# q, k and v cast to fp16 by GpSimd's DMA queue as they are loaded, in an attention kernel followed by a feed-forward network

## The chip, the cores and the metric

The kernel runs on one core of a Trainium2 chip. The metric is device time in microseconds of one execution; less is better. The kernel before was run three times: 346.05, 347.59 and 348.84 us, median 347.59.

## What is computed

Attention with a causal sliding window of 64 over 8 batches of 8 heads, 576 positions, head size 64, and then a feed-forward network with a squared ReLU on the 4608 resulting rows of 512:

```python
rel = pos[:, None] - pos[None, :]
mask = (rel >= 0) & (rel < 64)
scores = np.where(mask, q @ k.T / sqrt(64), -1e9)
attn = softmax(scores) @ v             # per batch and head
x = attn.transpose(0, 2, 1, 3).reshape(4608, 512)
h = np.maximum(x @ w_in, 0.0)          # w_in 512 x 2048
out = (h * h @ w_out)                  # w_out 2048 x 512
```

All inputs and the output are fp32 in memory; the kernel computes with fp16 operands.

## The kernel before, in words

The 4608 rows are 36 chunks of 128 positions, and four chunks are a group; there are nine groups. A chunk is two blocks of 64 positions. Each block of 64 queries needs 128 keys: its own block and the one before it.

A chunk goes through these functions. `load` (L144) brings k, q and v of the chunk, 128 positions x 8 heads x 64, from fp32 memory into three staging tiles of a pool of fifteen (`stage`), through DMAs on SP's queue (L151; for four of the chunks, which span two batches, in two halves at L154 and L156). GpSimd (POOL) then casts k and q to fp16 (L160, L162) and v to the tile `v_ev` (L164). The values of the first block of a chunk need v shifted by 64 positions, so two more POOL copies (L165, L167) put the lower half of `v_ev` into the upper half of `v_od` of this chunk, and its upper half into the lower half of `v_od` of the next. There are eight pairs of v tiles (`NV`) and eight fp16 tiles each for k and q. `transposes` (L169) turns k and q on TensorE and copies them to kT (DVE, L180, L177) and qT (ACT, L182). `scores` (L185) multiplies, takes the exponential on ACT (L199) and applies the mask as a minimum with 0 or 65504 on DVE (L201). `values` (L204) multiplies by v with a column of ones, and divides by the sum on DVE (L215, L216). `to_xT` (L221) transposes the result into xT (DVE, L226).

`ffn_up` and `ffn_up_chunk` multiply xT by w_in (TensorE L250, or L271 by single chunks), ReLU on ACT, squaring on DVE (L255, L276). `ffn_out` multiplies by w_out (L296), scales on ACT (L301) and stores through SP's queue (L303).

The weights are loaded as fp32 through SP's queue into four shared staging tiles (`ws`), w_in in 16 pieces of 256 KB (L115), cast on DVE (L117), and w_out in 16 pieces (L129), cast on POOL (L130). The masks are built by POOL in `base` (L75 to L80) and copied on DVE (L87). `warm` (L282) issues matmuls of no use for the result between the steps of chunk 0.

The program is written as one sequence: load of chunk 0, w_in, loads of chunks 1 to 6, the steps of chunk 0 with `warm` between them, load of chunk 7, w_out, then the steps of chunks 1 to 7 with their parts of the first product (L311 to L326), and from then on nine rounds (L329) in which `ffn_out` of one group, `ffn_up` of the next, `attention` of the one after and the loads two groups ahead are woven together. A scheduler of the language then orders the instructions of each engine by its own estimates, so that the order on an engine is not simply that of the text; it also places the waits. [...]

The functions that the diff touches:

Of the kernel before, what the change touches and what calls it, by code (L numbers as in the profile page):

```python
# [9 lines left out]
FP32 = mybir.dt.float32  # L10
FP16 = mybir.dt.float16
# [16 lines left out]
def kernel(  # L28
# [9 lines left out]
    nc = tc.nc  # L38
    B, H, S, D = q.shape
    NT, DM = out.shape  # L40
    DFF = moe_w_in.shape[1]
    P = 128
    HP = H // 2
    NCK = NT // P
    NB = S // 64
# [6 lines left out]

    const = ctx.enter_context(tc.tile_pool(name="const", bufs=1))
    wst = ctx.enter_context(tc.tile_pool(name="wst", bufs=4))
    stage = ctx.enter_context(tc.tile_pool(name="stage", bufs=15))
    st16 = ctx.enter_context(tc.tile_pool(name="st16", bufs=8))
    attw = ctx.enter_context(tc.tile_pool(name="attw", bufs=3))
    smallp = ctx.enter_context(tc.tile_pool(name="smallp", bufs=4))
# [18 lines left out]
        out=base[:], in_=base[:], compare_op=ALU.is_ge, fill=0.0, base=-1,  # L77
# [3 lines left out]
        out=base[:], in_=base[:], compare_op=ALU.is_ge, fill=0.0, base=64,  # L81
# [19 lines left out]
    NV = 8  # L101
    v_evs = [const.tile([P, H, 66], FP16, name=f"v_ev{i}") for i in range(NV)]
    v_ods = [const.tile([P, H, 66], FP16, name=f"v_od{i}") for i in range(NV)]
# [38 lines left out]
    q16s, k16s, qTs, kTs, pms, xs = {}, {}, {}, {}, {}, {}  # L142

    def load(i):  # L144

        sts = []
        for (src, nm) in ((k, "k"), (q, "q"), (v, "v")):
            st = stage.tile([P, H, D], FP32, name=f"{nm}_st", tag="st")
            b0, j0 = divmod(2 * i, NB)
            if j0 + 1 < NB:  # L150
                nc.sync.dma_start(  # L151
                    out=st[:], in_=src[b0, :, 64 * j0:64 * j0 + P, :].rearrange("h p d -> p h d"))
            else:
                nc.sync.dma_start(  # L154
                    out=st[0:64], in_=src[b0, :, 64 * j0:S, :].rearrange("h p d -> p h d"))
                nc.sync.dma_start(  # L156
                    out=st[64:P], in_=src[b0 + 1, :, 0:64, :].rearrange("h p d -> p h d"))
            sts.append(st)
        k16s[i] = st16.tile([P, H * D], FP16, name="k16", tag="k16")
        nc.gpsimd.tensor_copy(out=k16s[i][:], in_=sts[0][:].rearrange("p h d -> p (h d)"))  # L160
        q16s[i] = st16.tile([P, H * D], FP16, name="q16", tag="q16")
        nc.gpsimd.tensor_copy(out=q16s[i][:], in_=sts[1][:].rearrange("p h d -> p (h d)"))  # L162
        v_ev, v_od, v_next = v_evs[i % NV], v_ods[i % NV], v_ods[(i + 1) % NV]
        nc.gpsimd.tensor_copy(out=v_ev[:, :, 0:D], in_=sts[2][:])  # L164
        nc.gpsimd.tensor_copy(out=v_od[64:P, :, 0:D], in_=v_ev[0:64, :, 0:D])  # L165
        if i + 1 < NCK:
            nc.gpsimd.tensor_copy(out=v_next[0:64, :, 0:D], in_=v_ev[64:P, :, 0:D])  # L167

    def transposes(i):  # L169
        ps = ps_att.tile([P, 2, HP, P], FP16, name="qkT_ps", tag="ps_a")  # L170
        for s, src in enumerate((k16s, q16s)):
            for hp in range(HP):
                nc.tensor.transpose(out=ps[:, s, hp, :], in_=src[i][:, hp * P:(hp + 1) * P],  # L173
                                    identity=ident[:])
        kT = attw.tile([P, HP, 192], FP16, name="kT", tag="kT")
        if i > 0:
            nc.vector.tensor_copy(out=kT[:, :, 0:64], in_=kTs[i - 1][:, :, P:192])  # L177
        else:
            nc.vector.memset(kT[:, :, 0:64], 0.0)
        nc.vector.tensor_copy(out=kT[:, :, 64:192], in_=ps[:, 0])  # L180
        qT = attw.tile([P, HP, P], FP16, name="qT", tag="qT")
        nc.scalar.activation(out=qT[:], in_=ps[:, 1], func=AF.Copy, scale=1.0)  # L182
        kTs[i], qTs[i] = kT, qT
# [44 lines left out]
    def attention(g):  # L228

        steps = []  # L230
        fns = (transposes, scores, values, to_xT)
        for t in range(4 + len(fns) - 1):
            for s, fn in enumerate(fns):
                if 0 <= t - s < 4:
                    steps.append(lambda fn=fn, i=4 * g + t - s: fn(i))
        return steps

    def loads(g):
        return [lambda i=i: load(i) for i in range(4 * g, 4 * g + 4)]
# [69 lines left out]


    load(0)  # L311
    for s in load_w_in():
        s()
    NFIRST = 8
    for i in range(1, NV - 1):
        load(i)
    T, S_, V, X = [lambda i, fn=fn: fn(i) if i < NFIRST else None
                   for fn in (transposes, scores, values, to_xT)]
    T(0), warm(6), S_(0), warm(6), V(0), warm(6), X(0), warm(4)
    load(NV - 1)  # L320
# [48 lines left out]
```

The softmax here doesn't subtract the row's maximum and nothing guards it: scores larger than these inputs give would overflow.

## Time and profile before

| | |
|---|---|
| profiled execution, its span from first to last instruction | 345.9 us |
| three timed executions | 346.05, 347.59, 348.84 us |
| TensorE busy | 324.3 us (94%) |
| DVE busy | 207.9 us (60%) |
| ACT busy | 163.8 us (47%) |
| POOL busy | 121.5 us (35%) |
| DMA on SP's hardware queue, share of 16 engines | 51.7% |
| bytes moved | 46.65 MB |

The page gives no time for the profiled execution other than its span, so the span is set beside the three timed executions. PE is TensorE, PEld its weight loads, DVE VectorE, ACT ScalarE, POOL GpSimd, SP the engine that issues the DMAs; a q after the name is the engine's queue. In a slice view, each digit is the busy share of one fortieth of the span in tenths. In a timeline row, the first number is the start in us, the second the length in us; what stands in square brackets is the idle time before it and what ended it. L with a number is the line in the kernel.

### The profile page before, as it was taken

What the parts mean: (1) busy time and instruction counts of PE and PEld (TensorE: products, weight loads), DVE (VectorE), ACT (ScalarE), POOL (GpSimd) and SP (SyncE); (2) the same over time, 40 slices, a digit from 0 to 9 for tenths busy, and PEclk for the clock granted to TensorE, in tenths of its full rate; (3) what the DMA queues carried; (4) which work ended last, traced back from release to release, by engine and by line L of the source; (5) the groups of instructions that cost most, each with busy time, mean ns of one, the idle gap of its engine ahead of it and who ended that gap; (6) DMA issues with size and microseconds to landing.
All of it is one profiled execution on the core that took longest, in us unless ns stands there. A gap on an engine that the chain in (4) does not pass through costs nothing.

```text
span 345.9 us, 7917 instructions
## 1 busy us (share of the span) xinstructions
PE 324.3 (94%) x3146; PEld 178.2 (52%) x3146; DVE 207.9 (60%) x506; ACT 163.8 (47%) x289; POOL 121.5 (35%) x204
## 2 busy tenths in 40 slices
PE   1957888999999999999999999999999999999995
PEld 0346787875555555445545554455445544544442
DVE  2656988852666776676776657665675566544400
ACT  1123457544535646643664466436544654444411
POOL 4009895497753333316566544530000000000000
PEclk9996999999999999999999999999999999999998
DMA  7799987899972455546877757730011000000021
GB/s 200 249 252 239 234 247 252 207 230 228 243 172 61 93 121 123 121 124 155 212 185 182 170 135 184 185 87 27 23 45 36 30 32 32 30 30 32 35 88 62
DMA packets 122341, 46.65 MB, mean 135 GB/s; under 512 B 113600, under 2 KB 113600, under 8 KB 122304
## 3 DMA queue, kind: packets, MB, share of 16 engines
q1 hardware_dynamic: 122304, 46.15, 51.7%
q8 instruction: 24, 0.39, 0.5%
q14 instruction: 13, 0.11, 0.1%
HBM read 36.70 MB, written 9.44 MB: 133 GB/s over the span
## 4 chain that ended last, share of the span: by engine, by line
PE 83%; DVE 7%; DMA 5%; ACT 2%; SPq 1%; issue 1%; ACTq 0%
PE ops L296 37%; PE hps L250 28%; DMA ws<-in_moe_w_in_dram 5%; PE qkT_ps L173 4%; PE av L211 4%; PE xt_ps L224 2%; DVE h_397 L276 1%; DVE h_1087 L276 1%; DVE xT L226 1%; DVE w_in_sb L117 1%; PE hps_639 L271 1%; SPq L151 1%; SPq L115 0%; PE hps_1088 L271 0%; PE hps_1537 L271 0%
## 5 line engine op out<-in xcount | busy, mean ns | idle before, releaser
L250 PE MATMUL hps<-xT,w_in_sb 128*128 128x512 f16 x448 | 115.2, 379 | 0.0
L254 ACT ACTIVATE hrelu<-hps 128x512 f32<-128x512 f32 x112 | 66.8, 598 | 91.6 <-PE hps L250 90.9
L250 PEld LDWEIGHTS <-w_in_sb 128*128 128x128 f16 x448 | 43.7, 98 | 52.6 <-issue 0.3
L271 PEld LDWEIGHTS <-w_in_sb 128*128 128x128 f16 x512 | 31.2, 99 | 8.2 <-issue 3.9
L301 ACT ACTIVATE osb<-ops 128x512 f32<-128x512 f32 x36 | 21.6, 600 | 29.1 <-PE ops L296 28.9
L182 ACT ACTIVATE qT<-qkT_ps 128x512 f16<-128x512 f16 x36 | 21.5, 596 | 22.6 <-DVE kT L180 22.3
L216 DVE TENSOR_TENSOR x_sb<-av,rden 128x256 f16<-128x256 f32 x72 | 27.5, 415 | 0.1
L180 DVE COPY kT<-qkT_ps 128x512 f16<-128x512 f16 x36 | 15.2, 421 | 18.0 <-PE qkT_ps L173 17.8
L226 DVE COPY xT<-xt_ps 128x512 f16<-128x512 f16 x36 | 15.1, 420 | 12.7 <-PE xt_ps L224 12.7
L215 DVE RECIPROCAL rden<-av 128x4 f32<-128x4 f32 x72 | 11.4, 178 | 17.1 <-PE av L211 17.1
L255 DVE SCALAR_TENSOR_TENSOR h_5222<-hps,hrelu 128x512 f16<-128x512 f32 x16 | 11.1, 691 | 16.6 <-ACT hrelu L254 16.6
L296 PE MATMUL ops<-w_out_sb,h_1087 128*128 128x512 f16 x64 | 17.5, 380 | 0.0
L191 PEld LDWEIGHTS <-kT 64*128 64x128 f16 x576 | 11.0, 95 | 12.2 <-issue 9.6
L296 PE MATMUL ops<-w_out_sb,h_3120 128*128 128x512 f16 x64 | 16.5, 380 | 0.0
L296 PE MATMUL ops<-w_out_sb,h_2579 128*128 128x512 f16 x64 | 16.5, 380 | 0.0
L296 PE MATMUL ops<-w_out_sb,h_4199 128*128 128x512 f16 x64 | 16.5, 380 | 0.0
L296 PE MATMUL ops<-w_out_sb,h_3658 128*128 128x512 f16 x64 | 16.5, 380 | 0.0
L296 PE MATMUL ops<-w_out_sb,h_2041 128*128 128x512 f16 x64 | 16.5, 380 | 0.0
L296 PE MATMUL ops<-w_out_sb,h_4736 128*128 128x512 f16 x64 | 16.4, 379 | 0.0
L296 PE MATMUL ops<-w_out_sb,h_397 128*128 128x512 f16 x64 | 15.3, 380 | 0.0
L224 PE MATMUL xt_ps<-ident,x_sb 128*128 128x128 f16 x144 | 15.1, 222 | 0.1
L255 DVE SCALAR_TENSOR_TENSOR h_4736<-hps,hrelu 128x512 f16<-128x512 f32 x16 | 11.0, 689 | 6.8 <-ACT hrelu L254 6.4
(837 smaller groups left out, 611.1 us busy)
## 6 DMA issues: line engine op xcount, KB each, us to landing
out_dram<-osb SPq DMA_DIRECT2D x36, 256.0 KB, 2.2
k_st<-in_k_dram SPq DMA_DIRECT2D x32, 256.0 KB, 3.9
q_st<-in_q_dram SPq DMA_DIRECT2D x32, 256.0 KB, 4.0
v_st<-in_v_dram SPq DMA_DIRECT2D x32, 256.0 KB, 4.1
ws<-in_moe_w_in_dram SPq DMA_DIRECT2D x16, 256.0 KB, 4.2
k_st<-in_k_dram SPq DMA_DIRECT2D x8, 128.0 KB, 3.2
q_st<-in_q_dram SPq DMA_DIRECT2D x8, 128.0 KB, 3.0
v_st<-in_v_dram SPq DMA_DIRECT2D x8, 128.0 KB, 3.2
```

The lines of the kernel that those rows point to most:

```text
L173: nc.tensor.transpose(out=ps[:, s, hp, :], in_=src[i][:, hp * P:(hp + 1) * P], identity=ident[:])
L180: nc.vector.tensor_copy(out=kT[:, :, 64:192], in_=ps[:, 0])
L182: nc.scalar.activation(out=qT[:], in_=ps[:, 1], func=AF.Copy, scale=1.0)
L216: nc.vector.tensor_tensor(out=x_sb[:, 4 * half:4 * half + 4, :], in0=av[:, :, 0:D], in1=rden[:].to_broadcast([P, 4, D]), op=ALU.mult)
L224: nc.tensor.transpose(out=xt[:, c, :], in_=xs[i][:, 2 * c:2 * c + 2, :], identity=ident[:])
L226: nc.vector.tensor_copy(out=xT_of(i // 4)[:, :, (i % 4) * P:(i % 4 + 1) * P], in_=xt[:])
L250: nc.tensor.matmul(hps[:], w_in_sb[:, c, f * P:(f + 1) * P], xT_of(g)[:, c, :], start=(c == 0), stop=(c == DMC - 1))
L254: nc.scalar.activation(out=hrelu[:], in_=hps[:], func=AF.Relu)
L255: nc.vector.scalar_tensor_tensor(out=h2s[g][:, f, :], in0=hps[:], scalar=0.0, in1=hrelu[:], op0=ALU.max, op1=ALU.mult)
L271: nc.tensor.matmul(hps[:, f, :], w_in_sb[:, c, (4 * fq + f) * P:(4 * fq + f + 1) * P], xT_of(g)[:, c, t0:t0 + P], start=(c == 0), stop=(c ...
L296: nc.tensor.matmul(hold["ps"][:], h2s[g][:, f, ts * P:(ts + 1) * P], w_out_sb[:, f, :], start=(f == 0), stop=(f == FFC - 1))
L301: nc.scalar.activation(out=osb[:], in_=hold["ps"][:], func=AF.Copy, scale=OUT_SCALE)
```

## The change

k, q and v are no longer loaded as fp32 through SP's queue and cast by POOL instructions. The loads are issued on POOL's DMA queue with an fp16 destination, so that the cast happens in the transfer; v goes straight into `v_ev`. The two shifted copies of v become SBUF to SBUF transfers on SP's queue. The staging pool is gone. The transposes read k and q through a three-dimensional tile instead of a flat one.

```diff
-    stage = ctx.enter_context(tc.tile_pool(name="stage", bufs=15))
...
     def load(i):
 
-        sts = []
-        for (src, nm) in ((k, "k"), (q, "q"), (v, "v")):
-            st = stage.tile([P, H, D], FP32, name=f"{nm}_st", tag="st")
-            b0, j0 = divmod(2 * i, NB)
+        v_ev, v_od, v_next = v_evs[i % NV], v_ods[i % NV], v_ods[(i + 1) % NV]
+        k16s[i] = st16.tile([P, H, D], FP16, name="k16", tag="k16")
+        q16s[i] = st16.tile([P, H, D], FP16, name="q16", tag="q16")
+        b0, j0 = divmod(2 * i, NB)
+        for (src, dst) in ((k, k16s[i]), (q, q16s[i]), (v, v_ev[:, :, 0:D])):
             if j0 + 1 < NB:
-                nc.sync.dma_start(
-                    out=st[:], in_=src[b0, :, 64 * j0:64 * j0 + P, :].rearrange("h p d -> p h d"))
+                nc.gpsimd.dma_start(
+                    out=dst[:], in_=src[b0, :, 64 * j0:64 * j0 + P, :].rearrange("h p d -> p h d"))
             else:
-                nc.sync.dma_start(
-                    out=st[0:64], in_=src[b0, :, 64 * j0:S, :].rearrange("h p d -> p h d"))
-                nc.sync.dma_start(
-                    out=st[64:P], in_=src[b0 + 1, :, 0:64, :].rearrange("h p d -> p h d"))
-            sts.append(st)
-        k16s[i] = st16.tile([P, H * D], FP16, name="k16", tag="k16")
-        nc.gpsimd.tensor_copy(out=k16s[i][:], in_=sts[0][:].rearrange("p h d -> p (h d)"))
-        q16s[i] = st16.tile([P, H * D], FP16, name="q16", tag="q16")
-        nc.gpsimd.tensor_copy(out=q16s[i][:], in_=sts[1][:].rearrange("p h d -> p (h d)"))
-        v_ev, v_od, v_next = v_evs[i % NV], v_ods[i % NV], v_ods[(i + 1) % NV]
-        nc.gpsimd.tensor_copy(out=v_ev[:, :, 0:D], in_=sts[2][:])
-        nc.gpsimd.tensor_copy(out=v_od[64:P, :, 0:D], in_=v_ev[0:64, :, 0:D])
+                nc.gpsimd.dma_start(
+                    out=dst[0:64], in_=src[b0, :, 64 * j0:S, :].rearrange("h p d -> p h d"))
+                nc.gpsimd.dma_start(
+                    out=dst[64:P], in_=src[b0 + 1, :, 0:64, :].rearrange("h p d -> p h d"))
+        nc.sync.dma_start(out=v_od[64:P, :, 0:D], in_=v_ev[0:64, :, 0:D])
         if i + 1 < NCK:
-            nc.gpsimd.tensor_copy(out=v_next[0:64, :, 0:D], in_=v_ev[64:P, :, 0:D])
+            nc.sync.dma_start(out=v_next[0:64, :, 0:D], in_=v_ev[64:P, :, 0:D])
```

More of the change, by code (lines that the diff above doesn't have):

```diff
@@ L172, in transposes @@
             for hp in range(HP):
-                nc.tensor.transpose(out=ps[:, s, hp, :], in_=src[i][:, hp * P:(hp + 1) * P],
+                nc.tensor.transpose(out=ps[:, s, hp, :], in_=src[i][:, 2 * hp:2 * hp + 2, :],
                                     identity=ident[:])
```

## The prediction

> **What bounds the kernel now.** I read the busy shares in slices first, then busy time by stage, the chain, and the timelines of the start.
>
> The page's slices (tenths; first TensorE, then its clock and the DMA engines):
>
> ```profile
> PE   1957888999999999999999999999999999999995
> PEclk9996999999999999999999999999999999999998
> DMA  7799987899972455546877757730011000000021
> ```
>
> TensorE is full from about slice 9 on; the DMA engines are full only at the start. The table of stages makes it exact (stretch, length, then busy us of PE, PEld, DVE, ACT, POOL, then clock, DMA share, GB/s):
>
> ```profile
> 0.00:72.00 72.00, 54.78 (x850) 42.79 (x851) 50.52 (x139) 30.60 (x54) 40.23 (x73) 0.95 0.88 234
> 72.00:342.00 270.00, 269.54 (x2298) 135.44 (x2296) 157.35 (x367) 132.76 (x236) 81.31 (x132) 1.00 0.43 109
> ```
>
> From 72 us TensorE is busy 269.54 of 270 us: nothing gained or lost on POOL, SP or DVE there counts unless TensorE is made to wait. The time is therefore 72 (start) + 270 + 4 (tail), and the change is decided in the first 72 us. Their chain:
>
> ```profile
> 4.12 5.49 DMA ws<-in_moe_w_in_dram
> 10.09 4.25 DMA ws<-in_moe_w_in_dram
> 14.81 3.77 DMA ws<-in_moe_w_in_dram
> 19.72 5.40 DMA ws<-in_moe_w_in_dram
> 25.63 0.92 PE hps_506 L271 x13
> ```
>
> Four rounds of w_in loads (four staging buffers) carry it to 25.6 us. Then it runs TensorE, ACT, DVE, chunk after chunk, to 72 us, 6.4 us each, with DVE busy 4.1 to 4.8 of each 5 us from 35 us on. POOL's copies are hardly in it. Three events of DVE's timeline I need (start, length):
>
> ```profile
> 8.25 0.28 DVE L87 COPY mask_inner<-base 128x512 f16<-128x512 f16 x1
> ...
> 16.10 0.43 DVE L117 TENSOR_SCALAR w_in_sb<-ws 128x512 f16<-128x512 f32 x1 [0.32 <-DMA ws<-in_moe_w_in_dram]
> ...
> 40.89 0.82 DVE L201 TENSOR_TENSOR pm_765<-pm_765,mask_inner 128x512 f16<-128x512 f16 x1
> ```
>
> and one of TensorE's:
>
> ```profile
> 8.58 4.80 PE L286 MATMUL warm<-mask_inner,ident 128*128 128x512 f16 x12 [2.70 <-DVE mask_inner L87]
> ```
>
> The mask copies run after the first w_in cast; 16.10 is the ninth cast; the warm matmuls wait for mask_inner; and the L201 minimum takes 0.82 us there against 0.41 when POOL is quiet.
>
> [...]
>
> **What the change removes.** Per chunk five POOL instructions of 0.61 us (L160 to L167), some 180 in all; POOL is on no path after 72 us, so their own worth is nothing. What they do to DVE is worth something: the L201 minima between 27 and 72 us exceed 0.41 us by 3.3 us in sum (the fourteen durations less 14 x 0.41). DVE is nearly the limit there, so I count three quarters: -2.5 us, 1.0 of it before 38 us and 1.5 after. SP also loses its 120 loads; its first w_in issue moves from 2.73 to 0.82 us.
>
> **What it adds on POOL.** 120 loads (108, of which 12 are in halves). Each full one is 128 x 8 runs[...]. Price X: [...] I take X = 1.6 (a half 1.3).
>
> **What it moves.** The built instruction order of the changed kernel matters more than the diff. (a) DVE now has nine w_in casts ahead of the mask copies, before it was one, and twelve ahead of kT of chunk 0, before four. (b) TensorE has 3 + 12 warm matmuls ahead of chunk 0's scores, before 12. (c) Chunk 0's shift of v stands on SP behind fifteen of the sixteen w_in loads. (d) TensorE has two matmuls with w_out (L296 before) already behind chunk 2's transposes to xT; their casts stand on POOL behind 27 loads. Before, the first stood at 71.4 us.
>
> (a) and (b): ninth cast at 16.10, so mask_inner is done near 17.0 instead of 8.5. Fifteen warm matmuls at 0.40 (12 took 4.80) and the q transposes: scores of chunk 0 at 23.3, before 13.3. From there xT took 6.05 us; three interleaved warms fewer, 1.2 off: 28.2. Then four hps groups at the unhindered pace, 5.5 us: 33.7, where before stood at 27.0 (it had waited for w_in anyway). So +6.7. (c) The fifteenth w_in load was issued near 19 us, so the shift lands near 23, before chunk 0's values at 25: hidden, and worth its excess if w_in is later. The shift waits for v by POOL's third load, long done.
>
> w_in's pace itself: by 25 us the loads ahead would ask for 4.2 MB of w_in plus 15 x 0.26 MB, 8.1 MB; before moved 5.9 MB. At 285 GB/s, the best unsaturated stretch (10 to 15 us), 8.1 MB take 28.5 us, not 25. Against it stands SP's head start. At the ninth cast I take +1.5[...]; ends -3 and +8. Together +8.7.
>
> (d) POOL: 1.1 (memsets) + 21 x 1.6 + 6 x 1.3 + three selects (0.8) + two casts (1.2) = 44.5 us. TensorE comes there at 38.3 (end of that transpose before) + 8.7 - 1.0 = 46.0. Hidden, by 1.5 us; each 0.1 of X is 2.4 us, so this cover is gone at X = 1.7. The remaining fourteen w_out casts and twelve loads take 12 x 1.6 + 9 = 28 us, to about 73; TensorE's use begins near 79.
>
> After 72 us: twelve loads per group take 19 us of POOL against 30 us of TensorE (270/9), and a load runs a group ahead. Hidden up to X = 2.5. The 71 shifts of 512 runs go through SP, which waits for stores up to 8.5 us; their readers are a group, 30 us, away. DMA share there is 0.43. Hidden.
>
> Sum: 345.9 + 8.7 - 2.5 = 352.1 for the span. The three runs' median is 347.6, 1.7 above the profiled span, so I say 354.
>
> **Rivals.** *POOL's generator becomes the bound* (X above 2.3). Then (d) decides: at X = 2.3 (a half 1.65) TensorE stands until 61, 15 us beyond 46: 367 span, 369; at X = 3 until 78, 384 span, 386; above that the later stages run out of loads too, and X = 4 gives 432 us of POOL, some 500 in all. For: 1024 runs in every load[...]. *Delay and relief cancel*: if w_in keeps its pace and SP's head start holds, +6.7 - 1.9 - 2.5 = 348 span, 350. For: DMA share was only 0.7 in the first 10 us; against: POOL's loads start at once. *Faster*: rounds of w_in take 3.6 us (shortest landing 3.2, plus the 0.43 cast) instead of 4.7. Then nine casts are done near 11.5 and twelve soon after; chunk 0 reaches the end of hps near 27 as before, and the relief of 3.3 stays: 342.6 span, 344 or less. It decides below about 3.9 us a round; against it, every round before took longer with fewer loads beside it. That the casts don't leave POOL is excluded: the built order shows none but w_out's.
>
> **How the numbers follow.** Forecast case (X up to 2.3, start delayed), 351 to 367: 0.5. Generator: 0.24, 367 and beyond. Cancel, 345 to 351: 0.19. Faster, under 344: 0.07. One per cent is 3.5 us, about what a measurement here can tell. Faster 0.07, same 0.2, slower 0.73. Range: leaving the fast case and the worst half of the generator case out, 346 to 388. Likeliest alone: 351 to 367.
>
> **What would show it.** POOL's DMA rows give X directly. Right if mask_inner ends near 17 us, the first hps near 28, TensorE full from about 78, and later stages as before. L201 should read 0.41. Wrong if mask_inner ends before 12, if TensorE idles at L289 (the w_out matmul's new line) for many microseconds, or if it has gaps after 80 us.

## The result and the profile after

The changed kernel took 351.37 us (median of four runs, 350.12 to 353.43), the kernel before 347.35 us in four runs beside it: ratio 1.0116, 95% interval 1.0071 to 1.016. A second set of runs of the same kernel gave 352.52 us and 1.0119 (1.0076 to 1.0162). The change costs 1.2%. The profiled execution took 353.43 us, with a span of 351.7 us.

First the slices of the changed kernel, and its table of stages (columns as in the table shown for the kernel before):

```profile
PE   0086699999999999999999999999999999999995
PEclk9998989999999999999999999999999999999999
DMA  9999999999999958994999699961000000100021
```

```profile
0.00:72.00 72.00, 45.86 (x712) 36.00 (x713) 43.24 (x125) 25.85 (x46) 45.26 (x66) 0.95 1.63 203
72.00:78.00 6.00, 5.58 (x113) 5.27 (x113) 5.52 (x14) 4.00 (x8) 6.00 (x9) 1.00 1.92 131
78.00:346.00 268.00, 267.86 (x2318) 134.66 (x2315) 155.68 (x369) 133.68 (x236) 60.34 (x72) 1.00 0.71 79
```

TensorE is empty for two slices, where before it had worked in the first already. From 78 us it is busy 267.86 of 268 us: nothing is lost later. From the seventh store (the start of ACT's seventh copy of results out of PSUM) to the end of the span it is 224.6 us before, 224.3 after, and 224.2 to 224.7 in all the experiments. So everything happens before that store, and its time (121.28 us before, 127.36 after) compares kernels well. A DMA share above 1 means that the packets' times overlap, also within one queue: POOL's queue alone had 115% in the first 45 us.

What TensorE waited for up to 85 us (us in total, times, longest):

```profile
PE warm L279 <- DVE mask_inner L86: 10.0, 1, 10.0
PE qkT_ps L166 <- DMA k<-in_k_dram: 8.7, 1, 8.7
PE av L204 <- DMA v_od<-v_ev: 3.2, 1, 3.2
PE av L204 <- DVE pm L194: 2.6, 2, 1.9
...
```

The first k lands at 8.7 us, then TensorE stands until the masks are there. VectorE's timeline says why:

```profile
18.39 0.43 DVE L116 TENSOR_SCALAR w_in_sb<-ws 128x512 f16<-128x512 f32 x1 [1.64 <-DMA ws<-in_moe_w_in_dram]
18.73 0.29 DVE L86 COPY mask_first<-base 128x512 f16<-128x512 f16 x1
18.93 0.29 DVE L86 COPY mask_inner<-base 128x512 f16<-128x512 f16 x1
...
28.50 0.43 DVE L116 TENSOR_SCALAR w_in_sb<-ws 128x512 f16<-128x512 f32 x1 [0.86 <-DMA ws<-in_moe_w_in_dram]
28.84 0.76 DVE L194 TENSOR_TENSOR pm<-pm,mask_first 128x512 f16<-128x512 f16 x2
31.68 0.43 DVE L116 TENSOR_SCALAR w_in_sb<-ws 128x512 f16<-128x512 f32 x1 [2.09 <-DMA ws<-in_moe_w_in_dram]
32.02 0.24 DVE L208 RECIPROCAL rden<-av 128x4 f32<-128x4 f32 x2
...
33.56 0.42 DVE L219 COPY xT<-xt_ps 128x512 f16<-128x512 f16 x1 [0.57 <-PE xt_ps L217]
```

18.39 is the ninth cast of w_in (16.10 before), 31.68 the sixteenth (25.14 before). The mask copies are ready work of 0.3 us each, behind nine casts that wait for transfers: POOL's `base`, which they read, is finished at 4.06 us, but VectorE comes to them only at 18.73. And it doesn't end there. Chunk 0's minima (28.84) stand behind the fifteenth cast and its division (32.02) behind the sixteenth, so that chunk 0's xT follows w_in's last cast by 1.9 us; in the kernel before it was copied at 18.94, ahead of the last five casts. SP's queue and POOL's costs:

```profile
0.81 21.85 SPq L114 DMA_DIRECT2D ws<-in_moe_w_in_dram  x15
22.71 0.71 SPq L158 DMA_DIRECT2D v_od<-v_ev  x1
```

```profile
L151 POOL DMA_DIRECT2D q<-in_q_dram x32 | 28.8, 899 | 3.6 <-DMA v_ev<-in_v_dram 3.0 <-issue 0.3 <-PE hps L264 0.2
...
L156 POOL DMA_DIRECT2D k<-in_k_dram x4 | 2.8, 708 | 0.9 <-DMA v_ev<-in_v_dram 0.9
```

A full casting load takes 0.90 us of POOL, a half about 0.70. SP issues chunk 0's shift at 22.71 us, behind fifteen loads of w_in.

### The profile page after: what moved, and what is told of

It reads as the page before. It is cut to its first block, busy times and chain, and to the rows that moved or that the text cites. A ratio compares the mean times of both kernels' runs of the same rounds, so it can differ in the third digit from the quotient of the medians.

```text
span 351.7 us, 7866 instructions
## 1 busy us (share of the span) xinstructions
PE 321.1 (91%) x3146; PEld 176.5 (50%) x3146; DVE 204.4 (58%) x506; ACT 164.1 (47%) x289; POOL 111.6 (32%) x145
## 4 chain that ended last, share of the span: by engine, by line
PE 85%; DMA 7%; DVE 3%; ACT 2%; POOL 1%; issue 1%; POOLq 0%; ACTq 0%
PE ops L289 37%; PE hps L243 27%; PE hps L264 6%; PE qkT_ps L166 4%; PE av L204 4%; PE sc L184 3%; DMA q<-in_q_dram 3%; DMA v_ev<-in_v_dram 3%; PE xt_ps L217 2%; DMA v_od<-v_ev 2%; ACT hrelu L268 2%; DVE h L269 2%; DVE pm L194 1%; PE warm L279 1%; ACT qT L175 0%
## 5 line engine op out<-in xcount | busy, mean ns | idle before, releaser
L289 PE MATMUL ops<-w_out_sb,h 128*128 128x512 f16 x576 | 146.4, 380 | 0.0
L247 ACT ACTIVATE hrelu<-hps 128x512 f32<-128x512 f32 x112 | 66.9, 597 | 96.5 <-PE hps L243 95.8
L248 DVE SCALAR_TENSOR_TENSOR h<-hps,hrelu 128x512 f16<-128x512 f32 x112 | 77.2, 689 | 49.6 <-ACT hrelu L247 47.5
L289 PEld LDWEIGHTS <-h 128*128 128x128 f16 x576 | 49.4, 98 | 44.0
L151 POOL DMA_DIRECT2D v_ev<-in_v_dram x32 | 28.7, 896 | 54.3 <-PE av L204 52.3
L192 ACT ACTIVATE pm<-sc 128x512 f16<-128x512 f32 x72 | 39.0, 598 | 4.4 <-PE sc L184 4.2
L151 POOL DMA_DIRECT2D k<-in_k_dram x32 | 28.7, 898 | 34.1 <-PE qkT_ps L166 30.5
L264 PE MATMUL hps<-xT,w_in_sb 128*128 128x128 f16 x512 | 32.6, 222 | 1.4 <-DVE xT L219 0.7
L294 ACT ACTIVATE osb<-ops 128x512 f32<-128x512 f32 x36 | 21.6, 600 | 25.2 <-PE ops L289 25.2
L264 PEld LDWEIGHTS <-w_in_sb 128*128 128x128 f16 x512 | 30.2, 99 | 2.7 <-issue 2.1
L151 POOL DMA_DIRECT2D q<-in_q_dram x32 | 28.8, 899 | 3.6 <-DMA v_ev<-in_v_dram 3.0
L209 DVE TENSOR_TENSOR x_sb<-av,rden 128x256 f16<-128x256 f32 x72 | 26.9, 415 | 0.0
L268 ACT ACTIVATE hrelu<-hps 128x512 f32<-128x512 f32 x32 | 19.1, 597 | 15.5 <-PE hps L264 14.5
L194 DVE TENSOR_TENSOR pm<-pm,mask_inner 128x512 f16<-128x512 f16 x56 | 23.3, 433 | 4.3 <-ACT pm L192 3.7
L269 DVE SCALAR_TENSOR_TENSOR h<-hps,hrelu 128x512 f16<-128x512 f32 x32 | 22.0, 687 | 6.1 <-ACT hrelu L268 5.7
```

The costliest lines, as they stand in the source:

```text
L151: nc.gpsimd.dma_start(out=dst[:], in_=src[b0, :, 64 * j0:64 * j0 + P, :].rearrange("h p d -> p h d"))
L192: nc.scalar.activation(out=pm[:], in_=sc[hh][:], func=AF.Exp, scale=1.0 / float(D) ** 0.5)
L194: nc.vector.tensor_tensor(out=pm[:], in0=pm[:], in1=mask, op=ALU.min)
L209: nc.vector.tensor_tensor(out=x_sb[:, 4 * half:4 * half + 4, :], in0=av[:, :, 0:D], in1=rden[:].to_broadcast([P, 4, D]), op=ALU.mult)
L247: nc.scalar.activation(out=hrelu[:], in_=hps[:], func=AF.Relu)
L248: nc.vector.scalar_tensor_tensor(out=h2s[g][:, f, :], in0=hps[:], scalar=0.0, in1=hrelu[:], op0=ALU.max, op1=ALU.mult)
```

## The experiments

All of them, with the ratio to runs of the kernel before on the same chip. "xT 0, 1, 7" is when VectorE starts the copy of that chunk's xT, which begins its matmuls with w_in. The last column is the time before 120 us in which TensorE's clock was granted at one half, as far as the trace's record of the clock goes: it begins between 11.9 us (e4) and 25.4 us (e14).

| kernel | us, median | ratio (95%) | cast 16 | xT 0 | xT 1 | xT 7 | store 7 | half clock |
|---|---|---|---|---|---|---|---|---|
| before | 347.35 | 1 | 25.1 | 18.9 | 31.0 | 69.3 | 121.3 | 6.8 |
| changed | 351.37 | 1.0116 (1.0071-1.016) | 31.7 | 33.6 | 42.8 | 77.3 | 127.4 | 6.8 |
| changed, again (e12) | 352.52 | 1.0119 (1.0076-1.0162) | 30.4 | 32.2 | 41.1 | 74.0 | 124.0 | 3.4 |
| e1 | 348.2 | 1.0002 (0.9984-1.0021) | 32.9 | 21.6 | 37.4 | 71.6 | 122.1 | 17.1 |
| e5 | 354.86 | 1.0198 (1.0151-1.0245) | 25.2 | 26.9 | 44.8 | 80.5 | 130.9 | 20.5 |
| e6 | 354.35 | 1.0188 (1.014-1.0237) | 29.5 | 19.4 | 45.8 | 80.3 | 130.8 | 23.9 |
| e3 | 352.87 | 1.0143 (1.01-1.0186) | 28.6 | 33.7 | 43.2 | 78.4 | 128.8 | 13.7 |
| e4 | 358.95 | 1.0314 (1.0257-1.0372) | 28.0 | 17.9 | 33.2 | 77.5 | 133.1 | 20.5 |
| e7 | 346.94 | 0.9958 (0.9941-0.9975) | 30.5 | 22.9 | 34.9 | 70.5 | 120.9 | 13.7 |
| e9 | 347.96 | 0.9986 (0.9962-1.0011) | 30.2 | 22.4 | 36.8 | 71.8 | 122.2 | 13.7 |
| e11 | 347.06 | 0.9965 (0.9936-0.9993) | 29.2 | 21.2 | 35.8 | 69.9 | 120.3 | 10.2 |
| e10 | 355.46 | 1.0172 (1.0117-1.0228) | 29.8 | 31.5 | 40.3 | 75.5 | 126.0 | 3.4 |
| e13 (as e10) | 354.72 | 1.0185 (1.0152-1.0218) | 30.6 | 32.3 | 41.1 | 77.8 | 127.8 | 6.8 |
| e14 | 343.09 | 0.9852 (0.982-0.9883) | 28.8 | 21.1 | 34.4 | 69.3 | 119.4 | 10.2 |

The half clock comes in pieces of 3.41 us (one piece in e12, five in e1) and its place changes between executions of one kernel. The two profiles of the changed kernel are 3.3 us apart at the seventh store (127.4 and 124.0). So the times of a single profile are no better than about 3 us, and verdicts rest on the medians.

**e1, masks first.** Written with a hint for the order of instructions on an engine:

```diff
-            nc.vector.memset(m[0:64, :, first, :], 0.0)
+            last_mask[0] = nc.vector.memset(m[0:64, :, first, :], 0.0)
...
-            nc.vector.tensor_scalar(
-                out=w_in_sb[:, c, quar * FQ:(quar + 1) * FQ], in0=ws[:],
-                scalar1=W_SCALE, scalar2=None, op0=ALU.mult)
+            with tc.issue_after(last_mask[0].ins):
+                nc.vector.tensor_scalar(
+                    out=w_in_sb[:, c, quar * FQ:(quar + 1) * FQ], in0=ws[:],
+                    scalar1=W_SCALE, scalar2=None, op0=ALU.mult)
```

> The changed kernel with VectorE's three mask copies ordered ahead of all w_in casts (chunk 0's shift of v then also stands on SP behind 6 w_in loads, not 15). Theory: the start of the changed kernel is late by two delays side by side, the masks and the shift behind the casts, and the slower landing of w_in. Taking the first away leaves the second: warm matmuls start near 9 us (k has to land) and no longer near 19; the sixteenth cast stays near 31.7; chunk 0's hps end near 33.5 where they ended at 38.5; 346 to 348 us where the changed kernel had 351.4. Rival A, the late masks are hidden and only the slower w_in counts: hps of chunk 0 end near 38 still, 351. Rival B, the wait for the shift (3.2 us) is all that counts: 348, and the start gains 3.2 only.

348.2 us, just above the theory's 346 to 348 and as fast as the kernel before; its interval and the changed kernel's don't touch. The masks are copied from 4.09 us on, and chunk 0's xT at 21.55, long before the last cast. So the order on VectorE, chunk 0's work behind w_in's casts, is enough to explain what the change cost: without it the whole 1.2% is gone. Rival A falls. Rival B forecast the same time; e3 decides on it. The delay in landing stayed (sixteenth cast 32.9), and something new came: 17.1 us of half clock, and SP's queue:

```profile
0.81 6.05 SPq L116 DMA_DIRECT2D ws<-in_moe_w_in_dram  x6
10.25 0.70 SPq L161 DMA_DIRECT2D v_od<-v_ev  x1
...
11.82 7.63 SPq L116 DMA_DIRECT2D ws<-in_moe_w_in_dram  x5
```

SP stands from 6.86 to 10.25 us on the shift, until v of chunk 0 has landed, with ten w_in loads behind it.

**e3, the shift on POOL.**

```diff
-        nc.sync.dma_start(out=v_od[64:P, :, 0:D], in_=v_ev[0:64, :, 0:D])
+        nc.gpsimd.tensor_copy(out=v_od[64:P, :, 0:D], in_=v_ev[0:64, :, 0:D])
...
-            nc.sync.dma_start(out=v_next[0:64, :, 0:D], in_=v_ev[64:P, :, 0:D])
+            nc.gpsimd.tensor_copy(out=v_next[0:64, :, 0:D], in_=v_ev[64:P, :, 0:D])
```

> The changed kernel with the two shifts per chunk as POOL copies again (loads still cast by the DMA queue; VectorE's order of nine casts ahead of the masks unchanged). Theory: TensorE no longer waits 3.2 us for the shift at chunk 0's values; chunk 0's hps end near 35; the minima with masks beside POOL's copies take up to 0.8 us again, some 1 us in sum; 348 to 350 us. POOL waits for v of chunk 0 before it goes on to chunk 1's loads, so w_in may also be 1 or 2 us earlier. Rival, the shift only took the place of another wait (w_in): 351 to 353.

352.87 us: no gain, the rival was right, and Rival B of e1 falls. The wait for the shift is gone, and another stands in its place:

```profile
PE qkT_ps L166 <- DMA k<-in_k_dram: 9.0, 1, 9.0
PE warm L279 <- DVE mask_inner L86: 8.8, 1, 8.8
PE av L204 <- DVE pm L194: 5.8, 2, 4.2
```

Chunk 0's values start at 29.40 us, in the changed kernel at 29.52. The minima of chunk 0 stand on VectorE behind a late cast of w_in here too: this kernel's sixteenth cast is 3.1 us earlier (28.58), but the minima follow it (28.93). Two waits ended within about 0.1 us of each other, and the profile named only the last.

**e5 and e6, later loads held.** e5 holds the casting loads of chunks 1 to 6 behind one POOL copy that reads the last part of w_in; e6 is e1 and e5 together.

```diff
+    g_t = const.tile([P, 1], FP16, name="g_t")
+    gate = nc.gpsimd.tensor_copy(out=g_t[:], in_=w_in_sb[:, DMC - 1, DFF - 1:DFF])
-    for i in range(1, NV - 1):
-        load(i)
+    with tc.issue_after(gate.ins):
+        for i in range(1, NV - 1):
+            load(i)
```

> The changed kernel with the POOL loads of chunks 1 to 6 held until the last part of w_in is cast; VectorE's order unchanged (nine casts ahead of the masks). Theory: w_in landed late because the casting loads of later chunks share the DMA engines with it (its landing 5.7 us, before 4.2). Held back, the ninth cast comes near 15.5 and the sixteenth near 24.5 as in the kernel before, mask_inner near 16, the shift is issued near 17, chunk 0's hps end near 33; the loads that are held (0.9 us of POOL each) stay ahead of their readers, but w_out's first casts come near 44 us, just at their reader: 346 to 348 us. Rival, w_in is slow for another reason[...]: casts stay within 1 us of the changed kernel's, 351 or more.

> Both edits at once: masks ahead of the casts, and loads of chunks 1 to 6 held until w_in is cast. Theory: the two delays lie side by side, so either edit alone is stopped by the other, and both together bring back the start of the kernel before: chunk 0's hps end near 27, 340 to 343 us, if w_out's first casts (near 44 us) don't hold TensorE, which would come there near 38 to 40; with that wait 345 to 347. Rival, the delays are in series: each edit alone gives 3 to 4 us, both 7 to 8, 343 to 344, and either alone 347 to 348 with the other's whole delay still in the trace.

Half of it held. With the loads away, the casts are back at the pace of the kernel before; from VectorE's timeline of e5:

```profile
15.84 0.43 DVE L116 TENSOR_SCALAR w_in_sb<-ws 128x512 f16<-128x512 f32 x1 [0.57 <-DMA ws<-in_moe_w_in_dram]
...
25.17 0.43 DVE L116 TENSOR_SCALAR w_in_sb<-ws 128x512 f16<-128x512 f32 x1 [0.52 <-DMA ws<-in_moe_w_in_dram]
```

They came near the forecast (15.5 and 24.5), and show the second cause: casting loads beside it slow w_in (31.7, in e12 30.4, against 25.2). The median landing of a w_in load agrees: 5.8 us in the changed kernel, 4.4 in e5. Holding the loads holds POOL's instructions for them too (0.90 us each), but what the casts themselves lose is small: the sixteen exceed 0.43 us by 0.7 us in sum in the changed kernel and by 0.2 in e5. Chunk 0's xT again follows the last cast by 1.7 us (26.9), 6.7 us earlier than in the changed kernel. But both kernels got slower, and both forecasts of the time were missed: chunk 1's k is issued at 25.8 us in e5, and TensorE waits for it and for q, 3.9 us together (4.2 us for k in e6). 20 us of half clock follow. Whether the two delays lie side by side or in series isn't settled by the times of this pair, since the gate brought its own wait. The traces say how they are linked: with VectorE in the changed kernel's order, chunk 0's xT comes 1.7 to 1.9 us after w_in's last cast in five profiles (changed, e12, e10, e13, e5), so it is w_in's delay that chunk 0 gets, through the order; with the masks first (e1) it doesn't.

**e7, e9, e11: better starts.** e7 is e1 with the gate for chunks 3 to 6 only. e11 is e1 with the shifts of chunks 0 to 2 as POOL copies, so that none stands between w_in's loads on SP. e9 is both.

```diff
-        nc.sync.dma_start(out=v_od[64:P, :, 0:D], in_=v_ev[0:64, :, 0:D])
+        shift = nc.gpsimd.tensor_copy if i < 3 else nc.sync.dma_start
+        shift(out=v_od[64:P, :, 0:D], in_=v_ev[0:64, :, 0:D])
         if i + 1 < NCK:
-            nc.sync.dma_start(out=v_next[0:64, :, 0:D], in_=v_ev[64:P, :, 0:D])
+            shift(out=v_next[0:64, :, 0:D], in_=v_ev[64:P, :, 0:D])
```

> The changed kernel with masks ahead of the casts and the loads of chunks 3 to 6 only held until w_in's last cast; chunks 1 and 2 are loaded at once. Theory: holding all later chunks failed because chunk 1's k and q then came late; with chunks 1 and 2 free and 12 loads fewer beside w_in, the sixteenth cast comes near 28 (32.9 with masks alone, 25.2 with all held), chunk 0's hps end near 30, no wait for k of chunk 1, and the pace of the chunk stage stays near 5.8 us: seventh store near 118 to 119, 344 to 346 us. Rival, six early loads slow w_in as much as twenty-one, since the few under way at a time are what counts: sixteenth cast near 32, 348 us.

> The kernel of e7 (masks first, loads of chunks 3 to 6 held until w_in is cast), and the shifts of chunks 0 to 2 as POOL copies, so that SP issues all sixteen w_in loads without a shift between them. Theory: with masks first the shift of chunk 0 stands on SP behind six w_in loads and waits there for v (from 6.9 to 11.1 us in e7), and ten w_in loads wait behind it; on POOL it holds only later loads of chunks. Sixteenth cast near 27 to 28 (30.5 in e7), no wait of TensorE for the shift (3.3 us in e7), xT of chunk 1 near 32.5, seventh store near 118.5 (120.9 in e7): 343.5 to 345.5 us. Rival, w_in is held by its landing beside the casting loads and not by SP's wait: sixteenth cast stays near 30, 346.5 to 348 us.

> The same without the gate: masks first, shifts of chunks 0 to 2 as POOL copies, later loads not held by anything but POOL's own copies. Theory: POOL's copies wait for v of their chunk and so spread the loads by themselves; part of the gate's effect comes with it. Sixteenth cast 28 to 30 (32.9 with masks first alone), 344.5 to 347 us where masks first alone gave 348.2. Rival, the shift's wait on SP cost nothing, since the four staging buffers of w_in hold SP anyway: sixteenth cast 32 to 33, 348 us.

e7 came out at 346.94 us, a little above its forecast (344 to 346) and 0.4% faster than before, though with a sixteenth cast at 30.5 and not 28. e11 did as well, at the upper end of its forecast, with the sixteenth cast at 29.2 where e1 had 32.9. That speaks for a cost of SP's wait in w_in's pace, but it is one profile of each, and the intervals of e11 and e1 overlap a little. e9 missed: both together are no better than each, and its sixteenth cast (30.2) and time are what its rival said, for which SP's wait costs nothing. So this point is open. What holds e9 was not found; VectorE's order differs between these kernels too.

**e4, the shifts alone.** The kernel before with only its shifts as transfers on SP; loads stay staged on SP, and POOL casts.

```diff
-        nc.gpsimd.tensor_copy(out=v_od[64:P, :, 0:D], in_=v_ev[0:64, :, 0:D])
+        nc.sync.dma_start(out=v_od[64:P, :, 0:D], in_=v_ev[0:64, :, 0:D])
...
-            nc.gpsimd.tensor_copy(out=v_next[0:64, :, 0:D], in_=v_ev[64:P, :, 0:D])
+            nc.sync.dma_start(out=v_next[0:64, :, 0:D], in_=v_ev[64:P, :, 0:D])
```

> The kernel before with one part of the change only: the two shifts per chunk become SBUF to SBUF transfers on SP; k, q and v are still loaded by SP into staging tiles and cast by POOL (three copies of 0.61 us per chunk, not five). The built order keeps one w_in cast ahead of the masks, and TensorE's matmuls for w_in stand in nearly unbroken runs of 16 or 32 per chunk, as in the changed kernel. Theory: the start stays that of the kernel before (chunk 0's hps end near 27), and the quicker pace of the chunk stage in the changed kernel comes from the order of TensorE and VectorE, not from POOL's missing copies: from xT of chunk 1 to xT of chunk 7 34.5 to 35.3 us (before 38.3, changed 34.5), seventh store near 117.5, 343 to 345 us. Rival, the pace comes from POOL's missing copies: two of five are gone here, so 36.8 us for that stretch and 346 us. Rival, the shift as a transfer is itself late (it took 6.8 us at chunk 0 of the changed kernel): waits at values of 2 us or more, 348 or above.

358.95 us. The first two theories missed it; the last had "348 or above", but for waits at the values, and TensorE's only wait there up to 90 us is 0.6 us, for a minimum. From SP's waits up to 90 us:

```profile
SPq L165 <- POOL v_ev L164: 18.4, 8, 4.0
...
```

Each shift waits at the head of SP's queue for POOL's cast of v, and everything behind it waits too: 18.4 us in eight waits. This half of the change is by itself worse than the whole. How SP's waits reach TensorE isn't shown: up to 90 us no wait of TensorE for k, q or v of a later chunk is longer than 0.3 us; the chain of work that ended last runs through w_out's late loads and their casts from 69 to 86 us, and 20.5 us of half clock took 8.0 us of TensorE's busy time (2.5 in the kernel before, both by busy time in the half clock times one half). In the changed kernel the loads have left SP, and a shift that waits there holds only w_in (chunk 0) and w_out. On the pace this run says nothing.

**e10, e12, e13: what POOL's copies cost VectorE.** After chunk 0 the changed kernel is quicker: xT 1 to xT 7 takes 34.5 us, before 38.3. e10 and its repeat e13 put five POOL copies per chunk back, whose output nobody reads; e12 is the changed kernel beside e13.

```diff
+        for _ in range(5):
+            nc.gpsimd.tensor_copy(out=scr[:], in_=xTs[i // 4][:, :, i % 4 * P:i % 4 * P + P])
```

> The changed kernel with five more POOL copies (128 x 512, f16) per chunk 1 to 7, whose output nobody reads: as many POOL copies per chunk as in the kernel before, in the changed kernel's order of TensorE and VectorE. Question: the stretch from xT of chunk 1 to xT of chunk 7 fell from 38.3 to 34.5 us with the change. Theory: most of that is the order (TensorE in unbroken runs of 16 or 32 for w_in), and POOL's absence is worth 1 us or so through VectorE's minima: 35 to 36 us here, 351.5 to 353 us in all. Rival (the prediction's relief): POOL's copies slow VectorE, and it is the chain of that stretch: 37 to 38.3 us, 354 to 355 us.

> The changed kernel unaltered, once more, for a second profile and for times on the same chip as the next run. In the profiles so far the half clock came in pieces of 3.41 us (two in the changed kernel, five with masks first, one with the added POOL copies), so times of single profiles don't compare within 2 us. Expected: 350 to 352.5 us; mask_inner near 19, sixteenth cast near 31.7 and chunk 0's xT near 33.5 as in the first profile; the stretch from xT of chunk 1 to xT of chunk 7 34 to 36 us, as the half clock falls in it or not.

> The changed kernel with five idle POOL copies per chunk 1 to 7, again: its times were 355 us in three of four runs, and 352.0 in the profiled one, which had one piece of half clock. Theory (order): the copies cost VectorE's minima 1 us or so: median within 1.5 us of the changed kernel's beside it. Rival (relief): median 3 to 4 us above the changed kernel's beside it, and the stretch from xT of chunk 1 to that of chunk 7 at 37 us or more.

The medians of e13 and e12 are 2.2 us apart (354.72 and 352.52): between the two theories, with six runs of each that overlap (349.73 to 354.6, 353.25 to 356.56). The stretch from xT 1 to xT 7 in e12, e13 and the kernel before, by the columns of the table of stages, and then VectorE's minima with mask_inner in e12 and e13 (busy us, mean ns):

```profile
41.07:73.97 32.90, 31.43 (x629) 28.98 (x629) 29.90 (x75) 22.57 (x41) 22.04 (x31) 1.00 1.65 194
```

```profile
41.11:77.77 36.66, 33.11 (x629) 30.29 (x629) 33.23 (x76) 22.57 (x41) 29.11 (x44) 0.95 1.32 165
```

```profile
31.02:69.33 38.31, 34.13 (x631) 30.18 (x630) 32.27 (x77) 22.24 (x41) 27.60 (x46) 0.97 0.89 234
```

```profile
L194 DVE TENSOR_TENSOR pm<-pm,mask_inner 128x512 f16<-128x512 f16 x10 | 4.5, 475 | 1.4 <-ACT pm L192 1.2
```

```profile
L196 DVE TENSOR_TENSOR pm<-pm,mask_inner 128x512 f16<-128x512 f16 x10 | 6.6, 680 | 1.7 <-ACT pm L194 1.5
```

The busy time of VectorE grows by 3.3 us (29.90 to 33.23), with 2.1 more on these ten minima and 1.9 more on the two with mask_second, and the stretch grows by 3.8 us. One piece of half clock lies in it in e13 (clock 0.95) and none in e12 (1.00): at most half of 3.4 us of that is the clock, and 2.1 us stay, as the medians have it. The profile of e10, which was its fastest run, shows less: 35.2 us, also with one piece of half clock, so that 0.6 us stay. So VectorE's relief is worth 0.6 to 2.1 us of the recovery by the profiles and some 2 by the medians. The kernel before stands 5.4 us above e12, of it some 1.1 us of half clock (31.0 to 33.2); less the copies' 2.1, another 2.2 us remain, and more if they cost less. TensorE's busy time goes with them: 34.13 us, 33.0 less the clock, against 31.43 for nearly as many matmuls (631 and 629). In the kernel before, TensorE's matmuls with w_in are often broken by other kinds after 17 or fewer; in the changed kernel they mostly stand 32 in a row. That this order is the cause was not tried.

**e14, without warm matmuls.** e11 with all the warm matmuls left out; they feed nothing in the output.

> The kernel of e11 (masks first, shifts of chunks 0 to 2 on POOL) without the warm matmuls, which feed nothing in the output. In e1, e7, e9 and e11 chunk 0 is early, TensorE idles between warm matmuls and w_in's last casts, and three to five pieces of half clock of 3.41 us follow between 19 and 44 us. Question: do the warm matmuls call the half clock? If so, fewer pieces here (none to two), and the chunk stage runs undisturbed: 342 to 345 us. Rival, the half clock follows the first dense stretch of w_in matmuls after idleness, warm or not: as many pieces as in e11 (three) or more, 346 to 349 us.

343.09 us, 1.5% below the kernel before, the fastest kernel here, and within the forecast. But the half clock stayed, three pieces in e11 and in e14, so the reason that I had offered is wrong. The first matmuls with w_in even took nearly twice as long without the warm ones (3.60 us against 1.95, one profile of each), in e14 (first line) and e11:

```profile
21.74 3.60 PE L268 MATMUL hps<-xT,w_in_sb 128*128 128x128 f16 x32
21.69 1.95 PE L268 MATMUL hps<-xT,w_in_sb 128*128 128x128 f16 x32 [0.58 <-DVE xT L223]
```

That loss is covered, since TensorE then waits in both until 28.0 or later. The gain's cause is open: the two profiles are only 1.0 us apart (344.6 and 343.6), while the medians differ by 4.0; e11's profile was one of its faster runs (346.26, of 345.28 to 351.04), e14's its slowest.

## Why the forecast held, step by step

The forecast was 354 us and slower, most likely 351 to 367; measured 351.4 and 352.5, at the lower edge of that, where the rival "delay and relief cancel" begins. The mechanism of the forecast and not the rival's was found: chunk 0 does start late behind the casts, and e1 takes the loss away. But two sizes were off that cancel: the start was later than forecast, and more of it was won back.

- *(a), (b), masks behind nine casts.* Right. With its own +1.5 for w_in's pace the sum has the masks done at 18.5 us (17.0 without); they were at 19.2, in e12 at 18.1. Chunk 0's scores began at 24.7; the sum, with its +2.0 for pace and casts, had 25.3.
- *From the scores to xT.* The mis-sized step. The sum took the 6.05 us of the kernel before, less 1.2, so some 30 us for xT; it was copied at 33.56, because the minima and the division of chunk 0 stand behind the fifteenth and sixteenth casts. The sign "first hps near 28" was missed too: chunk 0's matmuls with w_in (their result is called hps) began at 34.0. They were over at 38.5 us, where the sum had 35.7 (27.0 + 8.7). In the kernel before they ended at 26.5 and not 27.0, so they are 11.9 us later, forecast 8.7.
- *w_in's pace.* +1.5 us at the ninth cast was forecast, 2.3 was measured (18.39 against 16.10) and 1.2 in e12. The 0.5 us that the sum had for longer casts was an estimate that no trace of before carries; the sixteen exceed 0.43 us by 0.7 us in sum, before by 0.1. The sum left out the sixteenth: 6.5 us later (5.2 in e12). Casting loads beside w_in are its cause (e5).
- *(c), the shift called hidden.* It shows as a wait of 3.2 us. SP issues it at 22.71 and it lands 6.8 us later, at 29.5, where 23 was forecast. It cost nothing all the same, for reasons that I did not name: the minima were as late (e3), and the division waits for the sixteenth cast.
- *X, and (d) w_out behind 27 loads.* I took X, POOL's time for a full load, as 1.6 us, an estimate that no trace of before carries; it is 0.90, and 0.70 for a half, so 512 runs more cost 0.2 us. But with X = 0.90 the sum would have POOL through 27 loads and two casts at 26 us, and it was at 40.3: from the tenth load on POOL stood idle before most loads until an earlier one had landed (1.00 us at the tenth, which began at 11.34), 14 us in all, a term that the sum lacks. TensorE used the first two w_out casts at 49.2 us: nine microseconds of cover, not 1.5. So the generator rival (POOL's own time for its loads as the bound), at 0.24, is far from this case: it needed X above 2.3.
- *Relief.* -2.5 us forecast, about 2 by the medians of e13 and e12, 0.6 to 2.1 by profiles. The ten minima with mask_inner took 475 ns each in e12, and 680 in e13 and 534 in e10, where five POOL copies per chunk run beside them. But L201's minima (L194 now) did not all fall to 0.41: two with mask_second took 1.0 us each, beside a load and two w_out casts on POOL; in e12 the same two took 0.42 us beside a load alone. What the sum lacked is the rest of the recovery: the start's 11.9 us were 8.0 at xT 7 and 6.1 at the seventh store.
- *After 72 us hidden.* Right: TensorE is full from 78 us, as the forecast said, and busy 267.86 of 268 us from there.

The start was 3.2 us too early in the sum, the recovery 3.3 us too small (5.8 from the end of chunk 0's hps to the seventh store, where 2.5 was forecast). In e12 the start is 10.6 us late and 7.9 are won back. The total holds to 1% because the two offset, and that is luck.

## What to carry to other kernels

When work moves to another queue, read the new order on every engine that waits for a transfer: here chunk 0's work behind w_in's waiting casts cost the whole 1.2% (e1), while POOL's 120 instructions for loads, 0.90 us for a full one, show in no wait of TensorE after the one for the first k. Go through the order to the end: the copies of 0.3 us were seen, the division behind the last cast was not. Before taking a wait away, ask which other wait ends at the same time: the shift's 3.2 us were worth nothing (e3), and half of the change alone was worse than all of it (e4). And a transfer that waits at the head of a queue held every load behind it here, for 3.4 us in e1 and 18.4 us in e4, so look for a queue whose later work is not urgent.

## What was not expected of the hardware

- TensorE's clock was at one half in pieces of 3.41 us, from one to seven in a kernel before 120 us, nearly all within the first 52 us, where TensorE still has idle stretches. The stretches were 6.8 us long in the kernel before, 3.4 in e12 and 17.1 in e1. They cost e1 6.5 us of TensorE's busy time and e12 1.7, by the sum of busy time times the missing share of the clock.

```profile
PEclk9995599999999999999999999999999999999999
```

- That is e1's row. What calls the half clock was not found: e5, where chunk 0 starts 5.3 us later than in e1, has even more of it (20.5 us).
- The rows show full clock where the record has not yet begun, up to 12.8 us before and 23.1 us in the changed kernel. Some durations there are those of the half clock: in the kernel before, four transposes of k took 0.61 us at 4.39 us and 0.39 at 17.40, and 0.61 in e14 at 32.30, where the record has one half; in the changed kernel three warm matmuls took 1.44 us at 19.27 (0.48 each) and five took 1.25 at 25.05 (0.25 each), and four took 1.89 at 30.93 (0.47 each), where the record has one half.
- A shift of 64 KB from SBUF to SBUF took 6.8 us to land at chunk 0 of the changed kernel, with a median of 7.0 in the first 45 us; the median was 2.4 us in the first 60 us of e4, where no casting loads ran beside it.
- In the first 45 us of the changed kernel the full casting loads had a median landing of 10.7 to 11.6 us, with 128 KB written each; the staged q and v of the kernel before took 4.5 and 4.2 us and wrote 256 KB, with the same fp32 read.
